# First block of a fused attention and feed-forward kernel: two head pairs normed together in column halves, five groups begun early, sums ahead of products

## The chip, the cores and the metric

The kernel runs on one core of a Trainium2 chip. The metric is the device time of one execution in microseconds, the median over several executions. An execution is also profiled: its span runs from the first to the last instruction of the program on the core, and its time is a little longer than the span.

## The reference

Batch 8, 8 heads, sequence 576, head width 64. Attention without softmax: for each batch and head `kv = k^T v` (64x64), then `out = q kv`, then every row of 64 is divided by its root mean square and scaled by `g_norm`. The heads are laid side by side to `x` of 4608 tokens by 512. A feed-forward layer follows.

```python
kv = np.einsum('bhsd,bhse->bhde', k, v)
out = np.einsum('bhsd,bhde->bhse', q, kv)
rms = np.sqrt(np.mean(out * out, axis=-1, keepdims=True) + 1e-06)
x = (out / rms * g_norm) ...            # heads side by side: 4608 x 512
h = x @ w_in                            # 512 x 2048
g = np.maximum(h, 0.0) + alpha * np.minimum(h, 0.0)
y = g @ w_out                           # 2048 x 512
```

## The kernel before

The 4608 tokens are cut into nine windows of 512 (`W`). The 8 heads are taken as four pairs of 128 columns, `j` 0 to 3, which are also the four chunks `c` of the 512 columns of `x`. The 2048 columns of `w_in` are 16 groups `g` of 128. All products are in fp16 with fp32 sums in PSUM. The order of every engine's work is the order in which the kernel writes it out: each engine runs its own instructions in that order and waits on semaphores of the others. An instruction that waits holds up all that is behind it on its engine.

Loads go through GpSimd's queue, which casts to fp16: q, k, v of batch 0 in halves of four heads, then `w_in` in four quarters of four groups each (`load_w_in`), then k and q of batch 1, a quarter of `w_out`, v of batch 1, the other three quarters of `w_out`, then batch 2. GpSimd issues them in that order, and may have only a few under way: from the ninth on, it waits for an earlier one to land.

For the first two windows the attention is done column-wise by pairs. `regroup` (L106) copies q or k on VectorE into the order that TensorE reads. `step_t` (L211, L220) transposes q of a pair by five products into PSUM and copies it to SBUF on VectorE. `step_kv` (L232, L236) makes kv of two pairs and masks it to two diagonal blocks. `step_ot` (L257, L263) multiplies to `ot_ps` (128 columns of the pair by 512 tokens) and squares it on ScalarE. `ssq_mm` (L273, L275, L278) sums the squares over each head's 64 columns by a product with the mask, then takes ln and exp on ScalarE to get `rstd`. `norm` (L284) multiplies `ot_ps`, `g` and `rstd` on VectorE to `xt`, the pair's chunk of `x`.

A group of the first layer (`m1_group`) is four products over `c` into a PSUM bank `h_ps` (L422), then `m1_evac`: relu of the negative on ScalarE (`m_sb`, L429) and a multiply-add on VectorE (`gt`, L431). The second layer sums 16 groups into a bank (`y_mm`, L444). [...]

The first window is the part that changes. Before, it does pairs 0 and 1, then pairs 2 and 3; it begins three groups on pairs 0 and 1 in the three `h` banks, ends them when pairs 2 and 3 are normed, and then does groups 3 to 15 one after the other. Around them stand `keep_warm` products (L196), which compute nothing that is used. After group 10 VectorE regroups k of batch 1, after group 12 `spread_g` makes a diagonal of `g` on VectorE (`diag`, L466) and spreads it by a product (`g_ps`, L470; `g_all`, L473), after group 14 VectorE regroups q of batch 1. Then the second layer of window 0 runs three output banks at a time, with the attention of batch 1 put between its products (`window_steps`): the transposes of pair 0 first, then `kv`.

Of the kernel before, what the change touches and what calls it, by code (L numbers as in the profile page):

```python
# [9 lines left out]
FP32 = mybir.dt.float32  # L10
FP16 = mybir.dt.float16
AF = mybir.ActivationFunctionType
ALU = mybir.AluOpType
# [4 lines left out]
def kernel(  # L18
# [11 lines left out]
    nc = tc.nc  # L30

    B, H, S, D = q.shape
# [3 lines left out]
    P = 128  # L36
    NPAIR = H // 2
    W = 512
# [6 lines left out]
    NF = D_FF // P  # L45
    NC = D_MODEL // P
    assert NC == NPAIR and 0 < REM < P
    inv_d = 1.0 / D
    NB_PE = 2

    const_p = ctx.enter_context(tc.tile_pool(name="constp", bufs=1))
    w_p = ctx.enter_context(tc.tile_pool(name="weights", bufs=1))
    xt_p = ctx.enter_context(tc.tile_pool(name="xt", bufs=2))
    xm_p = ctx.enter_context(tc.tile_pool(name="xm", bufs=3))
    qkv_p = ctx.enter_context(tc.tile_pool(name="qkv", bufs=1))
    attn_p = ctx.enter_context(tc.tile_pool(name="attn", bufs=2))
    gt_p = ctx.enter_context(tc.tile_pool(name="gt", bufs=2))
    ysb_p = ctx.enter_context(tc.tile_pool(name="ysb", bufs=4))
    ps_h = ctx.enter_context(tc.tile_pool(name="psh", bufs=3, space=bass.MemoryType.PSUM))
    ps_y = ctx.enter_context(tc.tile_pool(name="psy", bufs=1, space=bass.MemoryType.PSUM))  # L60
    ps_s = ctx.enter_context(tc.tile_pool(name="pss", bufs=1, space=bass.MemoryType.PSUM))
    ps_o = ctx.enter_context(tc.tile_pool(name="pso", bufs=1, space=bass.MemoryType.PSUM))
# [10 lines left out]
            name=nc.get_next_instruction_name(),  # L73
# [31 lines left out]
    def regroup(b, nm, h0=0, h1=H, eng=None):  # L105
        (eng or nc.vector).tensor_copy(  # L106
            out=bufs[b % NBUF][nm][:, :, h0:h1, :].rearrange("p t h d -> p h t d"),
            in_=stages[b % NBUF][nm][:, h0:h1],
        )

    def load_batch(b):
        for nm in ("q", "k", "v"):
            load(b, nm)
# [8 lines left out]
    ident = const_p.tile([P, P], FP32, name="ident")  # L122
# [10 lines left out]
    mask16 = const_p.tile([P, P], FP16, name="mask16")  # L133
# [5 lines left out]
    eps_t = const_p.tile([P, 1], FP32, name="eps_t")  # L139
# [6 lines left out]
    g2col = const_p.tile([P, 1], FP32, name="g2col")  # L146
# [28 lines left out]
    def w_in_blk(c, g):  # L175
        i, r = divmod(g, GW)
        return w_in_sb[i][:, c, r * P : (r + 1) * P]
# [15 lines left out]
    def keep_warm(n, pool=(ps_s, "s")):  # L193
        ps = pool[0].tile([P, W], FP32, name="warm_ps", tag=pool[1])
        for i in range(n):
            nc.tensor.matmul(out=ps[:], lhsT=mask16[:], rhs=warm16[:], start=True, stop=True)  # L196


    qts, kvs, xts = {}, {}, {}
# [4 lines left out]
            return lambda t: st[:, 2 * j : 2 * j + 2, t, :]  # L204
        return lambda t: st[:, t, 2 * j : 2 * j + 2, :]

    def step_t(b, j, pool=(ps_s, "s")):
        qs = pair_cols(b, "q", j)
        qt_ps = pool[0].tile([P, NT * P], FP16, name="qt_ps", tag=pool[1])
        for t in range(NT):  # L210
            nc.tensor.matmul(  # L211
                out=qt_ps[:, t * P : (t + 1) * P],
                lhsT=qs(t),
                rhs=ident16[:],
                is_transpose=True,
                start=(t == 0),
                stop=(t == NT - 1),
            )
        qts[b, j] = attn_p.tile([P, S], FP16, name="qt_sb", tag=f"qt{j}")
        nc.vector.tensor_copy(out=qts[b, j][:], in_=qt_ps[:, 0:S])  # L220

    def step_kv(b, j0=0, j1=NPAIR, pool=(ps_s, "s")):
        if j0 == 0:
# [18 lines left out]
    ots = {}  # L242
    xms = {}

    def xt_of(w, c):
        return xms[w][:, c, :] if w >= NB_PE else xts[w, c][:]

    def step_ot(w, j, pool=None):
        if pool is not None:
            ot_ps = pool[0].tile([P, W], FP32, name="ot_ps", tag=pool[1])  # L250
        else:
            ot_ps = ps_o.tile([P, W], FP32, name="ot_ps", tag=f"o{j % 2}")
        n0 = w * W
        while n0 < (w + 1) * W:
            b = n0 // S
            n1 = min((b + 1) * S, (w + 1) * W)
            nc.tensor.matmul(  # L257
                out=ot_ps[:, n0 - w * W : n1 - w * W], lhsT=kvs[b, j],
                rhs=qts[b, j][:, n0 - b * S : n1 - b * S], start=True, stop=True,
            )  # L260
            n0 = n1
        sq = attn_p.tile([P, W], FP16, name="sq_sb")
        nc.scalar.activation(out=sq[:], in_=ot_ps[:], func=AF.Square)  # L263
        ots[w, j] = (ot_ps, sq)
# [5 lines left out]
    def ssq_mm(w, j, pool=(ps_o, "o2")):  # L270
        ot_ps, sq = ots.pop((w, j))
        ssq_ps = pool[0].tile([P, W], FP32, name="ssq_ps", tag=pool[1])
        nc.tensor.matmul(out=ssq_ps[:], lhsT=mask16[:], rhs=sq[:], start=True, stop=True)  # L273
        rstd = attn_p.tile([P, W], FP32, name="rstd")
        nc.scalar.activation(  # L275
            out=rstd[:], in_=ssq_ps[:], func=AF.Ln, bias=eps_t[:], scale=inv_d,
        )
        nc.scalar.activation(out=rstd[:], in_=rstd[:], func=AF.Exp, bias=0.0, scale=-0.5)  # L278
        ots[w, j] = (ot_ps, rstd)

    def norm(w, j):
        ot_ps, rstd = ots.pop((w, j))
        xts[w, j] = xt_p.tile([P, W], FP16, name="xt", tag=f"xt{j}")
        nc.vector.scalar_tensor_tensor(  # L284
            out=xts[w, j][:], in0=ot_ps[:], scalar=g2col[:], in1=rstd[:],
            op0=ALU.mult, op1=ALU.mult,
        )


    TAIL = NB_PE * (S - W)  # L290
# [126 lines left out]

    gts = {}

    def m1_mm(h_ps, w, g, cs):  # L420
        for c in cs:
            nc.tensor.matmul(  # L422
                out=h_ps[:], lhsT=w_in_blk(c, g), rhs=xt_of(w, c),
                start=(c == 0), stop=(c == NC - 1),
            )

    def m1_evac(h_ps, w, g):
        m_sb = gt_p.tile([P, W], FP32, name="m_sb", bufs=3)
        nc.scalar.activation(out=m_sb[:], in_=h_ps[:], func=AF.Relu, scale=-1.0)  # L429
        gt = gt_p.tile([P, W], FP16, name="gt", tag=f"gt{g}")  # L430
        nc.vector.scalar_tensor_tensor(  # L431
            out=gt[:], in0=m_sb[:], scalar=beta_sb[:, g : g + 1], in1=h_ps[:],
            op0=ALU.mult, op1=ALU.add,
        )
        gts[w, g] = gt

    def m1_group(w, g):
        h_ps = ps_h.tile([P, W], FP32, name="h_ps", tag="h")
        m1_mm(h_ps, w, g, range(NC))
        m1_evac(h_ps, w, g)  # L440

# [17 lines left out]
            nc.sync.dma_start(out=rows[t], in_=y_sb[i : i + REM, :])  # L459

    g_all = const_p.tile([P, D], FP32, name="g_all")

    def spread_g():

        diag = const_p.tile([P, D], FP32, name="diag")
        nc.vector.tensor_scalar(  # L466
            out=diag[0:D], in0=ident[0:D, 0:D], scalar1=g2col[0:D], scalar2=None, op0=ALU.mult,
        )
        g_ps = ps_y.tile([P, D], FP32, name="g_ps", tag="y")
        nc.tensor.matmul(  # L470
            out=g_ps[:], lhsT=ones32[0:D], rhs=diag[0:D], start=True, stop=True,
        )
        nc.vector.tensor_copy(out=g_all[:], in_=g_ps[:])  # L473


    H_POOL = (ps_h, "h")
    keep_warm(10)
    regroup(0, "q", 0, HH)
    step_t(0, 0, H_POOL)
    step_t(0, 1, H_POOL)  # L480
    regroup(0, "k", 0, HH)
    keep_warm(4)
    step_kv(0, 0, 2)
    keep_warm(2)
    step_ot(0, 0)
    step_ot(0, 1)
    regroup(0, "q", HH, H)
    step_t(0, 2, H_POOL)
    step_t(0, 3, H_POOL)
    alpha_ps = ps_y.tile([P, NF], FP32, name="alpha_ps", tag="y")  # L490
    nc.tensor.matmul(
        out=alpha_ps[:], lhsT=alpha_row[:], rhs=ident[0:NF, 0:NF], is_transpose=True,
        start=True, stop=True,
# [3 lines left out]
    nc.vector.tensor_scalar(  # L497
        out=beta_sb[:], in0=alpha_ps[:], scalar1=-1.0, scalar2=1.0, op0=ALU.mult, op1=ALU.add,
    )
    regroup(0, "k", HH, H)  # L500
    ssq_mm(0, 0)
    keep_warm(3)
    ssq_mm(0, 1)
    norm(0, 0)
    keep_warm(3)
    step_kv(0, 2, 4)
    norm(0, 1)
    step_ot(0, 2, (ps_o, "o2"))
    step_ot(0, 3, (ps_y, "y"))
    load_batch(2)  # L510
    first = [ps_h.tile([P, W], FP32, name="h_ps", tag="h") for g in range(3)]
    m1_mm(first[0], 0, 0, (0, 1))
    ssq_mm(0, 2, (ps_s, "s"))
    for g in (1, 2):
        m1_mm(first[g], 0, g, (0, 1))
    ssq_mm(0, 3, (ps_o, "o0"))
    keep_warm(6, (ps_o, "o1"))
    norm(0, 2)
    norm(0, 3)
    for g in range(3):  # L520
        m1_mm(first[g], 0, g, (2,))
    keep_warm(2, (ps_o, "o1"))
    for g in range(3):
        m1_mm(first[g], 0, g, (3,))
        m1_evac(first[g], 0, g)
    for g in range(3, NF):
        m1_group(0, g)
        if g == 10:
            regroup(1, "k")
        if g == 12:  # L530
            spread_g()
        if g == 14:
            regroup(1, "q")
# [31 lines left out]
    for w in range(1, NW):  # L565
        steps = phase_steps(w + 1)
        for g in range(NF):
# [12 lines left out]
            if parts[0] == 0:  # L580
                pool, tag = ((ps_y, "y"), (ps_s, "s"))[a % 2 if w > 1 else 0]
                y = pool.tile([P, W], FP32, name="y_ps", tag=tag)
# [10 lines left out]
    for a in range(TPW):  # L593
        y = ps_h.tile([P, W], FP32, name="y_ps", tag="h")
# [33 lines left out]
```

## Time and profile before

| | |
|---|---|
| median of four runs | 302.3 us (301.56, 302.02, 302.57, 303.42) |
| the profiled execution | 302.57 us, span 300.6 us |
| mean granted TensorE clock | 0.990 |
| TensorE busy (matmul) | 284.4 us, 95% of the span |
| VectorE, ScalarE, GpSimd busy | 166.9, 153.0, 97.9 us |
| read from HBM, written | 36.71 MB, 9.44 MB |

The times of the lines below are those of one execution, the profiled one. Busy TensorE time counts overlapped products, so 95% does not say that it runs at its peak. The granted clock is the share of TensorE's full clock that the chip allowed in a stretch.

### The profile page before, as it was taken

To read this page: it belongs to the slowest core of one execution; us is meant where nothing else is said; L and a number is where in the kernel's file an instruction comes from. 1 tells how busy PE (TensorE), PEld (TensorE's weight loads), DVE (VectorE), ACT (ScalarE), POOL (GpSimd) and SP (SyncE) were. 2 spreads that over 40 slices of the span, in tenths; PEclk is the share of its full clock that TensorE was granted. 3 is DMA by queue.
4 is the path that set the end of the run, shared out by engine and by line. 5 is a ranking of instruction groups with operands and counts; after the bars stand their busy time and mean duration, and the time that the engine had idled before them with its cause. 6 is when DMAs were issued, how large, how long until landed. Compare 5 with 4: busy or idle time off the path is not lost.

```text
span 300.6 us, 4238 instructions
## 1 busy us (share of the span) xinstructions
PE 284.4 (95%) x1530; PEld 136.5 (45%) x1530; DVE 166.9 (56%) x255; ACT 153.0 (51%) x298; POOL 97.9 (33%) x109
## 2 busy tenths in 40 slices
PE   5889799889999999999999999999999999999993
PEld 2434254444554454445544544454445444444441
DVE  5548654587695458445954584368537743443200
ACT  1376317774684457435843663467347544434220
POOL 9923410546046615541556166315002200000000
PEclk9999899999999999999999999999999999999998
DMA  7999999999139954992399449926211411122133
GB/s 91 193 206 200 203 204 188 170 210 171 41 76 128 230 110 81 153 234 62 81 137 221 106 80 179 215 53 92 58 35 39 94 35 35 38 51 53 38 70 70
DMA packets 66068, 35.54 MB, mean 118 GB/s; under 512 B 32752, under 2 KB 61440, under 8 KB 66048
## 3 DMA queue, kind: packets, MB, share of 16 engines
q0 software_dynamic: 29664, 18.35, 43.5%
q1 hardware_dynamic: 36384, 16.93, 28.2%
q8 instruction: 12, 0.20, 0.3%
q14 instruction: 8, 0.07, 0.1%
HBM read 36.71 MB, written 9.44 MB: 154 GB/s over the span
## 4 chain that ended last, share of the span: by engine, by line
PE 87%; DVE 3%; ACT 3%; issue 2%; DMA 2%; POOL 2%; POOLq 0%; ACTq 0%
PE h_ps L422 39%; PE y_ps L444 37%; PE kv_ps L232 3%; PE otm_ps L340 2%; DMA vst<-in_v_dram 2%; DVE gt L431 1%; PE warm_ps L196 1%; ACT m_sb L429 1%; PE ssq_ps L273 1%; ACT rstd L275 1%; PE ya L444 1%; PE yb L444 1%; PE yc L444 1%; PE ot_ps L257 1%; DVE ksb L106 1%
## 5 line engine op out<-in xcount | busy, mean ns | idle before, releaser
L431 DVE SCALAR_TENSOR_TENSOR gt<-m_sb,beta_sb,h_ps 128x512 f16<-128x512 f32 x144 | 106.8, 745 | 82.3 <-ACT m_sb L429 81.2
L444 PE MATMUL y_ps<-w_out_sb,gt 128*128 128x512 f16 x528 | 134.9, 379 | 0.0
L429 ACT ACTIVATE m_sb<-h_ps 128x512 f32<-128x512 f32 x144 | 85.6, 597 | 92.1 <-PE h_ps L422 92.0
L422 PE MATMUL h_ps<-xm,w_in_sb 128*128 128x512 f16 x448 | 115.0, 379 | 0.0
L444 PEld LDWEIGHTS <-gt 128*128 128x128 f16 x576 | 56.0, 98 | 65.8 <-issue 1.5
L422 PEld LDWEIGHTS <-w_in_sb 128*128 128x128 f16 x576 | 55.2, 98 | 64.5 <-issue 4.9
L364 POOL TENSOR_TENSOR rg<-ss,g_all 128x512 f32<-128x512 f32 (+1 forms) x30 | 31.2, 1041 | 86.9 <-ACT ss L362 86.0
L422 PE MATMUL h_ps<-xt,w_in_sb 128*128 128x512 f16 x128 | 32.9, 395 | 2.1 <-DVE gt L431 2.1
L451 ACT COPY y_sb<-y_ps 128x512 f32<-128x512 f32 x33 | 19.2, 581 | 17.4 <-PE y_ps L444 17.4
L352 DVE TENSOR_REDUCE ss<-sqm_sb 128x8 f32<-128x512 f32 (+1 forms) x30 | 20.5, 682 | 9.6 <-ACT sqm_sb L346 9.5
L346 ACT ACTIVATE sqm_sb<-otm_ps 128x512 f32<-128x512 f32 (+1 forms) x30 | 17.8, 592 | 9.3 <-PE otm_ps L340 9.3
L373 DVE TENSOR_TENSOR xrow<-otm_ps,rg 128x512 f16<-128x512 f32 (+1 forms) x30 | 20.4, 681 | 3.6 <-POOL rg L364 3.6
L106 POOL COPY qsb<-qst 128x2560 f16<-128x2560 f16 x5 | 11.6, 2316 | 11.9 <-issue 9.3
L106 POOL COPY ksb<-kst 128x2560 f16<-128x2560 f16 x5 | 11.6, 2318 | 7.3 <-DMA kst<-in_k_dram 7.3
L196 PE MATMUL warm_ps<-warm,mask 128*128 128x512 f16 x30 | 9.7, 461 | 3.8 <-DVE eps_t L140 3.3
L340 PEld LDWEIGHTS <-qtm 128*128 128x128 f16 x120 | 9.2, 98 | 8.4 <-issue 1.5
L340 PE MATMUL otm_ps<-kv_sb,qtm 128*128 128x128 f16 x120 | 11.6, 219 | 1.2 <-DVE xm L314 1.2
L263 ACT ACTIVATE sq_sb<-ot_ps 128x512 f16<-128x512 f32 x8 | 4.5, 589 | 15.4 <-PE ot_ps L257 15.4
L232 PE MATMUL kv_ps<-vst,ksb 128*128 128x128 f16 x160 | 10.4, 219 | 1.1 <-DMA vst<-in_v_dram 0.6
L232 PEld LDWEIGHTS <-ksb 128*128 128x128 f16 x160 | 9.5, 98 | 4.1 <-DVE ksb L106 2.0
L284 DVE SCALAR_TENSOR_TENSOR xt<-ot_ps,g2col,rstd 128x512 f16<-128x512 f32 x8 | 6.0, 749 | 8.9 <-ACT rstd L278 8.9
L359 ACT ACTIVATE ss<-ss,eps_t 128x8 f32<-128x8 f32 (+1 forms) x30 | 9.0, 301 | 3.1 <-DVE ss L352 3.1
(62 smaller groups left out, 124.2 us busy)
## 6 DMA issues: line engine op xcount, KB each, us to landing
out_dram<-y_sb SPq DMA_DIRECT2D x72, 128.0 KB, 2.4
kst<-in_k_dram POOLq DMA_DIRECT2D x7, 320.0 KB, 7.9
qst<-in_q_dram POOLq DMA_DIRECT2D x7, 320.0 KB, 5.0
vst<-in_v_dram POOLq DMA_DIRECT2D x7, 320.0 KB, 9.8
w_in_sb<-in_moe_w_in_dram POOLq DMA_DIRECT2D x4, 512.0 KB, 10.2
w_out_sb<-in_moe_w_out_dram POOLq DMA_DIRECT2D x4, 512.0 KB, 15.3
kst<-in_k_dram POOLq DMA_DIRECT2D x7, 256.0 KB, 8.9
qst<-in_q_dram POOLq DMA_DIRECT2D x7, 256.0 KB, 6.5
```

Of the source, the lines that this page charges most:

```text
L106: (eng or nc.vector).tensor_copy(out=bufs[b % NBUF][nm][:, :, h0:h1, :].rearrange("p t h d -> p h t d"), in_=stages[b % NBUF][nm][:, h0:h1],)
L232: nc.tensor.matmul(out=kv_ps[:, j - j0, :], lhsT=ks(t), rhs=vs(t), start=(t == 0), stop=(t == NT - 1),)
L340: nc.tensor.matmul(out=ot_ps[:, 2 * j : 2 * j + 2, :], lhsT=qtms[b][:, t * NPAIR + j, :], rhs=kvs[b, j], start=True, stop=True,)
L346: nc.scalar.activation(out=sq[0:n], in_=ot_ps[0:n], func=AF.Square)
L352: nc.vector.tensor_reduce(out=ss[0:n], in_=sq[0:n], op=ALU.add, axis=mybir.AxisListType.X,)
L364: nc.gpsimd.tensor_tensor(out=rg[0:n], in0=ss[0:n].unsqueeze(2).to_broadcast([n, H, D]), in1=g_all[0:n].unsqueeze(1).to_broadcast([n, H, D ...
L373: nc.vector.tensor_mul(out=x[0:n], in0=ot_ps[0:n], in1=rg[0:n])
L422: nc.tensor.matmul(out=h_ps[:], lhsT=w_in_blk(c, g), rhs=xt_of(w, c), start=(c == 0), stop=(c == NC - 1),)
L429: nc.scalar.activation(out=m_sb[:], in_=h_ps[:], func=AF.Relu, scale=-1.0)
L431: nc.vector.scalar_tensor_tensor(out=gt[:], in0=m_sb[:], scalar=beta_sb[:, g : g + 1], in1=h_ps[:], op0=ALU.mult, op1=ALU.add,)
L444: nc.tensor.matmul(out=y[:], lhsT=gts[w, g][:, a * P : (a + 1) * P], rhs=w_out_blk(g), start=(g == 0), stop=(g == NF - 1),)
L451: nc.scalar.copy(out=y_sb[:], in_=y[:])
```

## The change

In the order in which it stands in the kernel:

- The copy of the transposed q of pair 1 goes from VectorE to ScalarE (`eng=nc.scalar`).
- The sums of squares of pairs 0 and 1 are put earlier in TensorE's order: that of pair 0 ahead of the transposes of pairs 2 and 3, that of pair 1 ahead of the regroup of k. The warm products become fewer (30 become 21), some in the bank `o2`.
- Pairs 2 and 3 are no longer squared, summed and normed one after the other with 512 tokens each, but together, 256 tokens of both at a time: `half_ot` and `half_ssq`. The squares of the first half are made on ScalarE, those of the second on VectorE by a copy and a multiply.
- Five groups are begun, not three: two in the banks `o0` and `o1`. Their products on pair 0 stand partly ahead of and partly between `half_ot` and `half_ssq`; those on pair 1 between the two sums. The products on pairs 2 and 3 are done in halves of 256 columns, for the first half of all five groups, then for the second, then the groups are evacuated.
- Groups 5 and 6 use the banks `s` and `y`; from group 7 on the three `h` banks rotate.
- `diag` is made right after the first five groups, not in `spread_g`.

```diff
-        nc.vector.tensor_copy(out=qts[b, j][:], in_=qt_ps[:, 0:S])
+        if eng is nc.scalar:
+            nc.scalar.copy(out=qts[b, j][:], in_=qt_ps[:, 0:S])
+        else:
+            nc.vector.tensor_copy(out=qts[b, j][:], in_=qt_ps[:, 0:S])
...
+    HW = W // 2
+
+    def half_ot(i, pool, eng=None):
+        ot_ps = pool[0].tile([P, 2, HW], FP32, name="ot_ps", tag=pool[1])
+        for u in range(2):
+            nc.tensor.matmul(
+                out=ot_ps[:, u, :], lhsT=kvs[0, 2 + u],
+                rhs=qts[0, 2 + u][:, i * HW : (i + 1) * HW], start=True, stop=True,
+            )
+        sq = attn_p.tile([P, 2, HW], FP16, name="sq_sb")
+        if eng is nc.vector:
+            o_sb = attn_p.tile([P, 2, HW], FP32, name="o_sb", tag="rg")
+            nc.vector.tensor_copy(out=o_sb[:], in_=ot_ps[:])
+            nc.vector.tensor_mul(out=sq[:], in0=ot_ps[:], in1=o_sb[:])
+        else:
+            nc.scalar.activation(out=sq[:], in_=ot_ps[:], func=AF.Square)
+        ots["half", i] = (ot_ps, sq)
+
+    def half_ssq(i, pool):
+        ot_ps, sq = ots.pop(("half", i))
+        ssq_ps = pool[0].tile([P, 2, HW], FP32, name="ssq_ps", tag=pool[1])
+        nc.tensor.matmul(out=ssq_ps[:], lhsT=mask16[:], rhs=sq[:], start=True, stop=True)
+        rstd = attn_p.tile([P, 2, HW], FP32, name="rstd")
+        ...                                        # Ln, Exp on ScalarE as in ssq_mm
+        for u in range(2):
+            if i == 0:
+                xts[0, 2 + u] = xt_p.tile([P, W], FP16, name="xt", tag=f"xt{2 + u}")
+            nc.vector.scalar_tensor_tensor(
+                out=xts[0, 2 + u][:, i * HW : (i + 1) * HW], in0=ot_ps[:, u, :],
+                scalar=g2col[:], in1=rstd[:, u, :], op0=ALU.mult, op1=ALU.mult,
+            )
...
-    step_t(0, 1, H_POOL)
+    step_t(0, 1, H_POOL, nc.scalar)
     regroup(0, "k", 0, HH)
-    keep_warm(4)
+    keep_warm(4, O2)
     step_kv(0, 0, 2)
-    keep_warm(2)
+    keep_warm(1, O2)
     step_ot(0, 0)
     step_ot(0, 1)
     regroup(0, "q", HH, H)
+    ssq_mm(0, 0)
     step_t(0, 2, H_POOL)
     step_t(0, 3, H_POOL)
...
+    ssq_mm(0, 1)
+    keep_warm(3)
     regroup(0, "k", HH, H)
-    ssq_mm(0, 0)
-    keep_warm(3)
-    ssq_mm(0, 1)
     norm(0, 0)
-    keep_warm(3)
+    keep_warm(2)
     step_kv(0, 2, 4)
-    norm(0, 1)
-    step_ot(0, 2, (ps_o, "o2"))
-    step_ot(0, 3, (ps_y, "y"))
     load_batch(2)
     first = [ps_h.tile([P, W], FP32, name="h_ps", tag="h") for g in range(3)]
-    m1_mm(first[0], 0, 0, (0, 1))
-    ssq_mm(0, 2, (ps_s, "s"))
-    for g in (1, 2):
-        m1_mm(first[g], 0, g, (0, 1))
-    ssq_mm(0, 3, (ps_o, "o0"))
-    keep_warm(6, (ps_o, "o1"))
-    norm(0, 2)
-    norm(0, 3)
+    first += [ps_o.tile([P, W], FP32, name="h_ps", tag=f"o{g}") for g in range(2)]
     for g in range(3):
-        m1_mm(first[g], 0, g, (2,))
-    keep_warm(2, (ps_o, "o1"))
-    for g in range(3):
-        m1_mm(first[g], 0, g, (3,))
-        m1_evac(first[g], 0, g)
-    for g in range(3, NF):
-        m1_group(0, g)
+        m1_mm(first[g], 0, g, (0,))
+    half_ot(0, (ps_s, "s"))
+    norm(0, 1)
+    half_ot(1, (ps_y, "y"), nc.vector)
+    for g in (3, 4):
+        m1_mm(first[g], 0, g, (0,))
+    half_ssq(0, O2)
+    for g in range(5):
+        m1_mm(first[g], 0, g, (1,))
+    keep_warm(1, O2)
+    half_ssq(1, O2)
+    for i in range(2):
+        for c in (2, 3):
+            for g, h_ps in enumerate(first):
+                m1_mm(h_ps, 0, g, (c,), slice(i * HW, (i + 1) * HW))
+                if (i, c) == (1, 3):
+                    m1_evac(h_ps, 0, g)
+    nc.vector.tensor_scalar(
+        out=diag[0:D], in0=ident[0:D, 0:D], scalar1=g2col[0:D], scalar2=None, op0=ALU.mult,
+    )
+    for g in range(5, NF):
+        m1_group(0, g, {5: (ps_s, "s"), 6: (ps_y, "y")}.get(g, H_POOL))
```

More of the change, by code (lines that the diff above doesn't have):

```diff
@@ L205, in pair_cols, with step_t @@
         return lambda t: st[:, t, 2 * j : 2 * j + 2, :]
-    def step_t(b, j, pool=(ps_s, "s")):
+    def step_t(b, j, pool=(ps_s, "s"), eng=None):
         qs = pair_cols(b, "q", j)
@@ L287, in norm @@
         )
+    HW = W // 2
[19 more added lines that the diff above has]
+        rstd = attn_p.tile([P, 2, HW], FP32, name="rstd")
+        nc.scalar.activation(
+            out=rstd[:], in_=ssq_ps[:], func=AF.Ln, bias=eps_t[:], scale=inv_d,
+        )
+        nc.scalar.activation(out=rstd[:], in_=rstd[:], func=AF.Exp, bias=0.0, scale=-0.5)
+        for u in range(2):
[5 more added lines that the diff above has]
+            )
     TAIL = NB_PE * (S - W)
@@ L418, with m1_mm @@
     gts = {}
-    def m1_mm(h_ps, w, g, cs):
+    def m1_mm(h_ps, w, g, cs, cols=slice(0, W)):
         for c in cs:
             nc.tensor.matmul(
-                out=h_ps[:], lhsT=w_in_blk(c, g), rhs=xt_of(w, c),
-                start=(c == 0), stop=(c == NC - 1),
+                out=h_ps[:, cols], lhsT=w_in_blk(c, g), rhs=xt_of(w, c)[:, cols],
+                start=(c == 0), stop=(c == NC - 1 and cols.stop == W),
             )
@@ L435, in m1_evac, with m1_group @@
         gts[w, g] = gt
-    def m1_group(w, g):
-        h_ps = ps_h.tile([P, W], FP32, name="h_ps", tag="h")
+    def m1_group(w, g, pool=(ps_h, "h")):
+        h_ps = pool[0].tile([P, W], FP32, name="h_ps", tag=pool[1])
         m1_mm(h_ps, w, g, range(NC))
@@ L461 @@
     g_all = const_p.tile([P, D], FP32, name="g_all")
+    diag = const_p.tile([P, D], FP32, name="diag")
     def spread_g():
[L465 to L468, printed above, removed]
         g_ps = ps_y.tile([P, D], FP32, name="g_ps", tag="y")
@@ L476 @@
     H_POOL = (ps_h, "h")
+    O2 = (ps_o, "o2")
     keep_warm(10)
@@ L499 @@
     )
+    ssq_mm(0, 1)
+    keep_warm(3)
     regroup(0, "k", HH, H)
-    ssq_mm(0, 0)
-    keep_warm(3)
-    ssq_mm(0, 1)
     norm(0, 0)
-    keep_warm(3)
+    keep_warm(2)
     step_kv(0, 2, 4)
-    norm(0, 1)
-    step_ot(0, 2, (ps_o, "o2"))
-    step_ot(0, 3, (ps_y, "y"))
     load_batch(2)
     first = [ps_h.tile([P, W], FP32, name="h_ps", tag="h") for g in range(3)]
-    m1_mm(first[0], 0, 0, (0, 1))
-    ssq_mm(0, 2, (ps_s, "s"))
-    for g in (1, 2):
-        m1_mm(first[g], 0, g, (0, 1))
-    ssq_mm(0, 3, (ps_o, "o0"))
-    keep_warm(6, (ps_o, "o1"))
-    norm(0, 2)
-    norm(0, 3)
-    for g in range(3):
-        m1_mm(first[g], 0, g, (2,))
-    keep_warm(2, (ps_o, "o1"))
-    for g in range(3):
-        m1_mm(first[g], 0, g, (3,))
-        m1_evac(first[g], 0, g)
-    for g in range(3, NF):
-        m1_group(0, g)
+    first += [ps_o.tile([P, W], FP32, name="h_ps", tag=f"o{g}") for g in range(2)]
+    for g in range(3):
+        m1_mm(first[g], 0, g, (0,))
[17 more added lines that the diff above has]
+        out=diag[0:D], in0=ident[0:D, 0:D], scalar1=g2col[0:D], scalar2=None, op0=ALU.mult,
+    )
+    for g in range(5, NF):
+        m1_group(0, g, {5: (ps_s, "s"), 6: (ps_y, "y")}.get(g, H_POOL))
         if g == 10:
```

## The prediction

> **What bounds the kernel now.** I read the page first, then the chain of waits around the change, then the stages of the run cut at the changes of the granted clock, then the timelines of the engines in the first block. The page says that the run as a whole belongs to TensorE:
>
> ```profile
> span 300.6 us, 4238 instructions
> PE 284.4 (95%) x1530; PEld 136.5 (45%) x1530; DVE 166.9 (56%) x255; ACT 153.0 (51%) x298; POOL 97.9 (33%) x109
> PEclk9999899999999999999999999999999999999998
> ```
>
> The fifth slice of the clock row, 30 to 37.5 us, is below full. The chain of waits shows what happens there (columns: start, us, what):
>
> ```profile
> 22.99 7.08 PE h_ps L422 x32
> ...
> 31.39 0.82 DVE ksb L106
> 32.21 1.32 DVE gt L431 x2
> 33.53 0.17 DVE diag L466
> ...
> 33.73 0.43 PE g_ps L470 x2
> 34.17 4.40 PE h_ps L422 x12
> ...
> 40.38 1.29 PE kv_ps L232 x20
> ```
>
> VectorE regroups k of batch 1, then makes gt 11 and 12, then diag; TensorE, which ran out of work after group 12, waits for diag (1.95 us by the list of waits). Then twelve products take 4.40 us, though four take 0.86 elsewhere. The stages, cut at the clock's changes, say why (columns: stage, its length, PE, PEld, DVE, ACT and POOL busy, granted clock, DMA):
>
> ```profile
> 31.57:34.98 3.41, 1.46 (x9) 0.71 (x8) 2.34 (x5) 0.60 (x1) 1.59 (x2) 1.00 1.36 199
> 34.98:38.40 3.42, 3.42 (x10) 1.21 (x9) 1.61 (x3) 1.19 (x2) 1.35 (x2) 0.50 1.26 206
> 58.87:62.29 3.42, 2.22 (x17) 1.19 (x16) 2.48 (x4) 2.35 (x5) 1.61 (x3) 1.00 1.20 184
> ```
>
> TensorE was busy 1.46 of 3.41 us (43%), and the next stage of the same length ran at clock 0.50. A stage with 2.22 busy (65%) had no such sequel. So the limit lies between 43% and 65%; half clock over 3.41 us costs 1.7 us of full TensorE work. The profiled execution (302.57 us, span 300.6) holds this loss once. It lies 0.27 us above the median of the four runs, 302.3; the runs lie 1.86 us apart, about what one such loss is worth, so I take the executions to differ in it.
>
> What releases the first block is the arrival of the weights, to be read from GpSimd, which waits for one of its transfers before it issues the next:
>
> ```profile
> 17.09 0.77 POOL L169 DMA_DIRECT2D w_out_sb<-in_moe_w_out_dram  x1 [1.74 <-DMA w_in_sb<-in_moe_w_in_dram]
> 19.62 0.69 POOL L96 DMA_DIRECT2D vst<-in_v_dram  x1 [1.76 <-DMA w_in_sb<-in_moe_w_in_dram]
> ```
>
> The first quarter of w_in (groups 0 to 3) is there at about 16.8 us, the second (groups 4 to 7) at about 19.35. The wait sits some 0.28 us ahead of each issue: 9.31 + 7.5, the shortest landing of w_in, is 16.81.
>
> **The change, part by part.** Durations are rows of the profile: a 512-column product every 0.216 (four in 0.86), Ln 0.68, Exp 0.63, gt 0.75, but 0.66 from start to start where gts are ready (three in 2.06), m_sb 0.60. A half norm (128x256) is not in the trace. By the kv_sb rows (512 columns 0.692, 256 columns 0.424) a half saves 0.27, so 0.48 against the 0.75 of the whole; the bounds are 0.38 (half) and 0.75. A half product is 0.11 (half of 0.216). ScalarE's copy of qt_sb is bounded by 0.45 (VectorE's) and 0.65 (ScalarE's y_sb copy, scaled to 576 columns), VectorE's copy of o_sb from below by 0.45 and from above by 0.69 (kv_sb at 512). None of these three is on the path: the copies end before 10 and 19.7 us, and their readers wait for weights or for ssq.
>
> *Up to 16.8 us: nothing.* The qt copy on ScalarE, the earlier sum, the warm products taken out (30 become 21) let TensorE finish kv of pairs 2 and 3 near 15.0, where it now ends at 15.7. But the next instruction in TensorE's queue is now the product of group 0 on pair 0, which needs the first quarter: TensorE stands until 16.9. What is queued behind it is half_ot(0). Today the ot of pairs 2 and 3 start at 16.24, ahead of the weights; then they start at 16.9 + 3 x 0.216 = 17.55, a loss of 1.3 us.
>
> *16.9 to 24.6 us.* The four half ot end at 18.0; Square (0.59) ends at 18.6. TensorE does group 3, then reaches the c = 0 product of group 4 and stands until the second quarter, 19.45. Behind it waits the first half's sum: 19.67, its result 20.05. Today that sum starts at 17.32. Ln and Exp end at 21.45, the two half norms, 0.40 apart, at 22.35. The second sum follows five products and a warm one (19.9 + 1.3 = 21.2, result 21.6); Ln, Exp, 22.95; half norms at 23.45 and 23.85. TensorE has the ten half products of the first half done by then and does the second half from 23.5, pair 3 from 24.05 to 24.6. The first m_sb starts at 24.35 and the first gt at 24.97, against 22.19 now. But five groups are then done, not three: TensorE starts group 5 at 24.6 and ends it at 25.5, where it is today as well (its m_sb starts at 25.78).
>
> *24.6 to 38.6 us.* TensorE is level, VectorE is late: gt k starts at 24.97 + 0.66 k, diag takes 0.11 more after gt 4. Groups 5 to 9 have free PSUM banks and end at 28.9. Group 10 takes the bank of group 7, whose gt ends at 24.97 + 4.62 + 0.11 + 0.75 = 30.45: a new stall of 1.6 us. Then gt is no longer behind. Groups 10 to 12 end at 33.1; diag is long there, so the wait of 1.95 us is gone; g_ps takes 0.43; group 13 ends at 34.4. VectorE: gt 10 until 32.9, ksb until 33.7, gt 11 until 34.3, gt 12 until 35.0; group 14 and 15 pass with no wait above 0.1, and the first y product starts at 36.1 (38.37 now). Next late is VectorE again: gt 14 until 36.8, qsb until 37.5, then the transposes of pair 0, gt 15 until 38.2, the copy of qt until 38.6, and kv of batch 1 starts at 38.6 instead of 40.38. **The sum so far: 1.8 us earlier, clock untouched.**
>
> *What the 1.8 us meets.* GpSimd's queue issues the same transfers in the same order, each as an earlier one lands; DMA moves 184 to 206 GB/s in the stages quoted, from 31 us to 62, so landings stay. v of batch 1 is issued at 19.62 and 22.17, longest landing 15.5: by 37.7, in time. v of batch 2, second part, 39.28 + 13.7 (the median of these early ones) = 53.0, needed at 55.40 - 1.8 = 53.6: covered by 0.6 us; if the cover goes, the gain shrinks one for one. SP's transpose of q follows its regroup. Behind that, up to the end, TensorE is the bound, so the shift stays: 302.57 - 1.8 = 300.8.
>
> *The clock.* TensorE now stands from 15.0 to 16.9 and from about 18.2 to 19.45. In the profiled execution's stages (14.50 to 17.92), it would be busy some 1.5 of 3.41 us, 44 to 49%; a stage that holds both gaps has 2.1 us idle, 38% busy, less than the 43% that dropped. A drop in 17 to 21 us doubles the product of group 4, the first sum, the five products and the second sum: about eight products of 0.216, of which the part inside the stage counts, 0.6 to 1.7 us by where it lies, 0.9 in the profiled execution's. That gives 301.4 to 302.5, likeliest 301.6.
>
> The row says that a gap of 1.95 us is enough to lose the clock. [...]
>
> **The rivals.** (a) *The clock holds* through 15 to 21 us, because the limit is nearer to 43% or the gaps fall into two stages: 300.8, and 300.1 with shorter half norms and a shorter stall. For it: 44 to 49% lies above the one stage that dropped. Against: every stage that holds both gaps lies below it. (b) *Slower: a second drop at the bank stall.* TensorE idle from 28.9 to 30.5 leaves a stage around it 53% busy; if the limit is above 53%, as 65% allows, the next 3.4 us run at half clock and cost 1.7 more: 301.7 + 1.7 = 303.4, up to 304.5 where the first drop costs its most. It decides from a stall of 1.2 us (65% busy) if the limit is there. Against: 53% is nearer to the middle than either row. (c) *No difference*: VectorE or the v of batch 2 takes the gain back, 302.4; for it, the cover of 0.6 us only.
>
> **How the numbers follow.** The forecast has 0.38, (a) 0.36, (b) 0.19, (c) 0.07. The bound of what a measurement tells from no change, 0.5%, is 1.5 us: 300.8 and 303.8. Faster: 0.27 of (a), which lies at this bound and takes all that my sums count too long, and 0.02 of the forecast: 0.29. Slower: 0.14 of (b). Within: 0.57. The range leaves out 0.08 of (a) below 300.4 and 0.11 of (b) above 303.6. The forecast's own range is 301.2 to 302.5.
>
> **What would show it.** Right: first gt near 25 us, group 10 waiting for a gt near 29, no wait for diag, y from 36 to 37, kv of batch 1 from 38.6 to 39.7, clock 0.50 once near 17 to 21 and not after 33. Wrong: the sum of the first half before 19.4, an ot of pair 2 before 16.8, or kv of batch 1 after 40.4.

## The result, and the profile after

| | before | after |
|---|---|---|
| median of the runs shown with the result | 302.13 us (79 runs, 301.16 to 304.33) | 301.52 us (53 runs, 300.71 to 302.72) |
| profiled execution, span | 302.57, 300.6 us | 301.03, 299.0 us |
| first gt of the first block | 22.19 | 25.07 |
| first product of the second layer (y) | 38.37 | 36.28 |
| kv of batch 1, of batch 2, of batch 3 (first product) | 40.38, 55.40, 77.66 | 38.81, 53.82, 76.08 |

The ratio is 0.9972, with a 95% interval from 0.9964 to 0.998: faster by 0.28%, within the 0.5% that counts as no change here. Ratios here and below come from comparable runs on the same chip, so they are not the quotients of the medians. The shift at kv of batch 1, 1.57 us in the two profiled executions, is still there at batch 2 (1.58), at batch 3 (1.58) and in the span (1.6).

The page of the kernel after (span; busy time, share and instructions of each engine; the granted clock in 40 slices):

```profile
span 299.0 us, 4244 instructions
PE 281.5 (94%) x1533; PEld 136.4 (46%) x1533; DVE 167.1 (56%) x258; ACT 153.0 (51%) x298; POOL 97.6 (33%) x109
PEclk9999999999999999999999999999999999999999
```

TensorE has three instructions more and is busy 2.9 us less: the clock row has no slice below its highest digit (9 is 90% or more). The chain of waits of the kernel after, from the weights to kv of batch 2 (start, us, what):

```profile
10.05 9.21 DMA w_in_sb<-in_moe_w_in_dram
19.30 0.39 PE h_ps L461
19.69 0.22 PE ssq_ps L314
...
25.07 3.38 DVE gt L470 x5
...
30.63 2.75 PE h_ps L461 x12
33.38 0.36 PE g_ps L506 x2
33.75 1.85 PE h_ps L461 x8
...
53.82 1.29 PE kv_ps L235 x20
```

The first half's sum runs behind the product of group 4, which is what the second quarter of w_in releases at 19.30. The five evacuations then stand in a row on VectorE. At 33.38 `g_ps` follows the products of groups 10 to 12 with nothing between: the wait for `diag` is gone, and eight products behind it take 1.85 us, where twelve took 4.40 at half clock. TensorE's timeline of the kernel after shows the two gaps in front of the weights and the stall at group 10 (start, us, line, operation, tiles, count; in brackets the idle time before it and its releaser):

```profile
13.46 1.46 PE L196 MATMUL warm_ps<-warm,mask 128*128 128x512 f16 x5
14.98 0.72 PE L235 MATMUL kv_ps<-vst,ksb 128*128 128x128 f16 x10
16.80 0.82 PE L461 MATMUL h_ps<-xt,w_in_sb 128*128 128x512 f16 x3 [1.11 <-DMA w_in_sb<-in_moe_w_in_dram]
...
19.30 0.39 PE L461 MATMUL h_ps<-xt,w_in_sb 128*128 128x512 f16 x1 [1.03 <-DMA w_in_sb<-in_moe_w_in_dram]
19.53 0.38 PE L314 MATMUL ssq_ps<-sq_sb,mask 128*128 128x512 f16 x1
...
30.63 2.75 PE L461 MATMUL h_ps<-xt,w_in_sb 128*128 128x512 f16 x12 [1.47 <-DVE gt L470]
```

The stages of the kernel after that hold these gaps, cut like those of before (stage, its length, PE, PEld, DVE, ACT and POOL busy, granted clock, DMA):

```profile
14.48:17.89 3.41, 2.25 (x19) 1.34 (x18) 1.36 (x3) 0.63 (x2) 1.44 (x2) 1.00 1.24 207
17.89:21.30 3.41, 2.32 (x12) 0.84 (x10) 1.38 (x2) 1.90 (x3) 0.69 (x1) 1.00 1.24 206
28.13:31.54 3.41, 1.94 (x10) 0.82 (x9) 3.41 (x7) 2.15 (x4) 1.66 (x3) 1.00 1.34 203
```

TensorE is busy for 66%, 68% and 57% of them, and the clock stays at 1.00 behind each.

### The profile page after: what moved, and what is told of

It reads as the page before. It is cut to its first block, busy times and chain, and to the rows that moved or that the text cites. A ratio compares the mean times of both kernels' runs of the same rounds, so it can differ in the third digit from the quotient of the medians.

```text
span 299.0 us, 4244 instructions
## 1 busy us (share of the span) xinstructions
PE 281.5 (94%) x1533; PEld 136.4 (46%) x1533; DVE 167.1 (56%) x258; ACT 153.0 (51%) x298; POOL 97.6 (33%) x109
## 4 chain that ended last, share of the span: by engine, by line
PE 83%; DVE 4%; POOL 3%; ACT 3%; DMA 3%; issue 2%; POOLq 0%; ACTq 0%
PE y_ps L483 38%; PE h_ps L461 37%; DMA w_in_sb<-in_moe_w_in_dram 3%; PE kv_ps L235 3%; PE otm_ps L379 2%; DVE gt L470 2%; PE yc L483 1%; PE yb L483 1%; PE ya L483 1%; ACT m_sb L468 1%; PE qt_ps L211 0%; POOL qst L96 0%; ACT rstd L278 0%; PE ssq_ps L276 0%; POOL qst L100 0%
## 5 line engine op out<-in xcount | busy, mean ns | idle before, releaser
L461 PEld LDWEIGHTS <-w_in_sb 128*128 128x128 f16 x586 | 55.8, 98 | 66.0 <-issue 4.9
L461 PE MATMUL h_ps<-xt,w_in_sb 128*128 128x512 f16 (+1 forms) x138 | 31.6, 364 | 5.4 <-DVE gt L470 2.6
L196 PE MATMUL warm_ps<-warm,mask 128*128 128x512 f16 x21 | 7.6, 498 | 3.3 <-DVE eps_t L140 3.3
L239 DVE TENSOR_TENSOR kv_sb<-kv_ps,mask 128x512 f16<-128x512 f32 (+1 forms) x9 | 5.6, 628 | 4.1 <-PE kv_ps L235 4.0
L96 POOL DMA_DIRECT2D vst<-in_v_dram x9 | 6.6, 728 | 2.9 <-DMA w_in_sb<-in_moe_w_in_dram 1.7
```

What stands on the lines that cost most here:

```text
L461: nc.tensor.matmul(out=h_ps[:, cols], lhsT=w_in_blk(c, g), rhs=xt_of(w, c)[:, cols], start=(c == 0), stop=(c == NC - 1 and cols.stop == W),)
```

## The experiments

The questions were: which part of the change brings the gain (`diag`, or the new order of the first block); what half clock is worth and what sets it off; and what limits the gain further on. The first four are cut so that each does or undoes one thing.

### 1. `diag` alone

Before, with `diag` made behind the first three groups, and nothing else of the change:

```diff
-        nc.vector.tensor_scalar(out=diag[0:D], ...)    # in spread_g, after group 12
+    nc.vector.tensor_scalar(out=diag[0:D], ...)        # ahead of the loop over groups 3 to 15
```

> The kernel before, with diag made right after the first three groups and nothing else changed. Theory D (the gain is diag's: its wait of 1.95 us and the clock lost behind it go, and the new first block by itself costs): TensorE goes from group 12 to g_ps with no wait, y starts near 34.6, kv of batch 1 near 37.1 (40.38 before, 38.81 after), then kv of batch 2 stands until its v lands at 53.0, so that only some 0.9 us are left against an undropped run of before: median 300.6 us, 1.5 below before's and 0.9 below the changed kernel's. Theory B (the new first block brings the gain, diag is by the way): between before and after, 301.8 us.

Measured: 301.14 us (12 runs, 300.44 to 303.64), ratio 0.9954 [0.9933, 0.9975]. The one small instruction brings about as much as the whole change: the intervals of the two overlap. The profiled execution, 302.33, shows where it ends. Its load stream ran late (`w_in`'s first quarter is there at 18.7 us where it is at 16.6 to 17.5 in the others), and yet the y products begin at 36.52. Then the chain of waits is one of transfers up to kv of batch 2 (start, us, what):

```profile
12.79 14.34 DMA w_in_sb<-in_moe_w_in_dram
27.41 13.56 DMA w_out_sb<-in_moe_w_out_dram
41.25 13.83 DMA vst<-in_v_dram
55.21 1.28 PE kv_ps L232 x20
```

Each is issued when an earlier one lands; v of batch 2 lands last. TensorE was at kv of batch 1 by 39.05 us, 1.33 ahead of before, and is 0.19 ahead at kv of batch 2.

### 2. The change without its `diag`

After, with `diag` put back into `spread_g` (the diff above, the other way round).

> The changed kernel with diag back in spread_g, behind gt 12 on VectorE. Theory D: TensorE waits for diag again, longer than before since VectorE is later (its gts started 2.9 us later): y near 38.2, kv of batch 1 near 40.7, median 303.0 us and up to 304.5 where the clock drops, slower than before by 0.9 or more. Theory B: 301.5 to 302.0 us, still faster than before.

Measured: 304.99 us (7 runs, 304.18 to 305.33), ratio 1.0065 [1.0042, 1.0088]: slower than before. The chain of waits of this kernel (start, us, what):

```profile
32.95 0.82 DVE ksb L106
33.77 1.31 DVE gt L470 x2
35.09 0.17 DVE diag L505
35.30 0.43 PE g_ps L509 x2
35.73 4.38 PE h_ps L461 x12
```

Since gt runs later in the new block, `diag` behind two gts and the regroup is later too, 35.09 against 33.53, and the wait drops the clock as it did before. Its stages:

```profile
32.90:36.31 3.41, 1.46 (x8) 0.60 (x6) 2.57 (x6) 0.81 (x2) 1.36 (x2) 1.00 1.36 201
36.31:39.72 3.41, 3.41 (x9) 1.21 (x8) 1.14 (x2) 1.19 (x2) 0.94 (x2) 0.50 1.24 207
```

1.46 of 3.41 us busy, then 0.50: the same pair of rows as in the kernel before. But an earlier stage of the same execution, into which most of both gaps in front of the weights falls, is as little busy (1.47 us, 43%), and the clock holds behind it:

```profile
15.82:19.24 3.42, 1.47 (x8) 0.70 (x8) 2.11 (x4) 0.60 (x1) 0.76 (x1) 1.00 1.24 206
19.24:22.65 3.41, 2.94 (x16) 1.49 (x17) 1.23 (x3) 2.15 (x4) 1.08 (x2) 1.00 1.24 207
```

The y products start at 39.95, 1.58 later than before. So the new first block by itself costs time at that point, and `diag` pays for it.

### 3. The wait kept, the clock held

Before, with eight warm products put into the wait:

```diff
         if g == 12:
+            keep_warm(8, (ps_o, "o1"))
             spread_g()
```

> The kernel before with eight warm products ahead of g_ps, in the time in which TensorE waits for diag. If the clock's drop behind the wait is what spreads the runs of before (301.2 to 304.3): the wait for diag stays at some 0.2 us of idle with 1.7 us of useless products, the clock stays at 1.00 from 35 to 38 us, y starts near 36.7, and the runs lie at 301.5 us with none above 302.5. If the spread has another cause: median 302.1 us and the same spread as before.

Measured: 301.92 us (12 runs, 301.47 to 302.45), ratio 0.9975 [0.9957, 0.9993]. TensorE's timeline and the stage behind the wait, of this kernel:

```profile
31.77 1.89 PE L196 MATMUL warm_ps<-warm,mask 128*128 128x512 f16 x8
33.89 0.43 PE L470 MATMUL g_ps<-diag,ones 64*128 64x64 f32 x2 [0.23 <-DVE diag L466]
```

```profile
34.98:38.40 3.42, 3.10 (x15) 1.15 (x14) 2.33 (x4) 1.79 (x3) 2.13 (x3) 1.00 1.26 206
```

`g_ps` starts no earlier than before (33.89), only the clock behind it is full, and kv of batch 1 comes at 39.38 instead of 40.38: the drop costs 1.0 us there. From 39.38 to the 38.81 of the kernel after, 0.57 us are left for all else that the change does. This splits the spread of before as well. Of its 87 executions beside these experiments, 42 have a mean granted clock of 0.9945 or less and a median of 303.17 us; 45 have 0.9975 or more and a median of 302.07; none lie between. With the warm products none is above 302.45. Of the kernel after, 4 of 54 are at 0.9945 or less, and the other 50 have a median of 301.46. The mean clock also counts half clock behind the last product, where it costs nothing (the last 2.8 us of the span in the profile of before), so those 4 are the most that can have had a drop. So about 0.6 us of the gain does not depend on the drop, and about 1.1 us more is there against the half of the executions of before that have it.

### 4. The sums ahead of the products that wait for weights

After, with the ot of both halves ahead of the products on pair 0, and the first sum right behind the four products that the first quarter of `w_in` allows:

```diff
-    for g in range(3):
-        m1_mm(first[g], 0, g, (0,))
     half_ot(0, (ps_s, "s"))
     norm(0, 1)
     half_ot(1, (ps_y, "y"), nc.vector)
-    for g in (3, 4):
+    for g in range(4):
         m1_mm(first[g], 0, g, (0,))
     half_ssq(0, O2)
-    for g in range(5):
+    for g in range(4):
         m1_mm(first[g], 0, g, (1,))
     keep_warm(1, O2)
     half_ssq(1, O2)
+    m1_mm(first[4], 0, 4, (0, 1))
```

> The changed kernel with TensorE's order in the first block changed alone: half_ot ahead of the products on pair 0, which wait for the first quarter of w_in; the products of group 4, which wait for the second quarter, behind both sums. Theory Q (the new block's cost is what its sums wait for in TensorE's queue, the two quarters): the first sum starts near 18 us instead of 19.53, the first gt near 23.1 instead of 25.07, the bank stall at group 10 shrinks, y near 34.2, kv of batch 1 near 36.8; then v of batch 2 binds at 53.0: median 300.6 us. Theory H (the halves themselves, more and shorter instructions, are the cost): first gt 24.5 or later, median 301.3 us or more.

Measured: 301.44 us (12 runs, 300.29 to 302.96), ratio 0.9954 [0.9933, 0.9976]. In the first block it does what was expected: the first gt at 23.18 us (25.07 after), y at 34.39 (36.28), kv of batch 1 at 36.91 (38.81). Little of these 1.9 us is left in the time. TensorE's timeline of this kernel, and the stages around the second line:

```profile
17.77 0.38 PE L314 MATMUL ssq_ps<-sq_sb,mask 128*128 128x512 f16 x1
...
53.51 2.12 PE L235 MATMUL kv_ps<-vst,ksb 128*128 128x128 f16 x20 [1.95 <-DMA vst<-in_v_dram]
```

```profile
50.31:53.73 3.42, 1.48 (x11) 0.65 (x10) 2.23 (x3) 2.05 (x5) 0.00 (x0) 1.00 1.34 183
53.73:57.14 3.41, 3.41 (x27) 2.58 (x25) 0.69 (x1) 0.60 (x1) 1.14 (x3) 0.50 1.05 239
```

The sum moves from 19.53 to 17.77, and the 1.9 us come back as a wait of 1.95 us for v of batch 2. In this execution that wait drops the clock in its turn (mean clock 0.993; so in four of the twelve, 302.2 to 303.0 us; the other eight have a median of 300.86, so there some of the gain is left). v of batch 2 lands at 53.4 us here (issued at 39.04, 14.33 us to landing) and at 53.0 in the kernel after, although TensorE is 1.9 us earlier at kv of batch 1, so what is won ahead of 53.4 us ends there.

### 5, 6, 7. The consumer of that load moved back

kv of batch 2 two steps later in window 1, in the kernels of 1 and 4 and in the kernel after:

```diff
-            steps[0][1].append(lambda: step_kv(w))
+            steps[2 if w == NB_PE else 0][1].append(lambda: step_kv(w))
```

> The kernel before with diag early, as in the first of these runs, and in window 1 step_kv of batch 2 in the third step instead of the first, two groups later. Theory L (with diag early the kernel stands at kv of batch 2 until the last v of batch 2 lands, 53 to 55 us by the execution, and that is what caps every gain in the first block): the stand goes, kv of batch 2 runs near 54 with groups done ahead of it, and the median falls to 299.1 us, with less spread. Rival K (the chain behind kv, ScalarE, VectorE and GpSimd from 56 to 68 us, takes it back): 300.6 us or more.

> The changed kernel with the sums first in TensorE's queue, as in the fourth of these runs, and step_kv of batch 2 two groups later. Theory L: 298.8 us, 0.3 below the run with diag alone and the same move, which is what the new first block is worth once its queue order is mended. Rival K: 300.6 us or more. If the new first block is worth nothing even so: the same as the run with diag alone, within 0.2.

> The changed kernel with step_kv of batch 2 two groups later and nothing else. Theory L: its kv of batch 2 starts at 53.8 us, about when the last v lands, so the landing hardly binds and the move gives little: 0.3 to 0.5 us, median 301.1. Rival: the move itself is the gain wherever it is made: 299.5 us.

| | kv of batch 1 | span | median | ratio |
|---|---|---|---|---|
| 5: `diag` alone, kv later | 37.74 | 298.5 | 300.45 us (6 runs) | 0.9924 [0.9898, 0.9951] |
| 6: sums first, kv later | 37.13 | 298.0 | 300.36 us (6 runs) | 0.9925 [0.9899, 0.9952] |
| 7: after, kv later | 39.33 | 299.2 | 301.17 us (12 runs) | 0.9962 [0.9944, 0.998] |

Number 7 gains next to nothing over the kernel after, whose kv of batch 2 did not wait for v (a wait of 0.4 us in front of it is for VectorE's regroup). Numbers 5 and 6 beat both kernels, and they are level: the new first block with its order mended is worth nothing measurable over `diag` alone. They fell short of what was expected, 299.1 for number 5. The chain of waits of number 5 shows the next limit (start, us, what):

```profile
56.42 0.18 POOL gate L555
...
56.92 0.69 POOL qst L96
...
60.33 0.68 POOL vst L100
61.01 1.85 POOL rg L364 x2
```

GpSimd waits at its gate until the transposes of q of batch 2 are there, issues six transfers of batch 3, and only then multiplies `rg` for the rows of the next window. Number 6 has the same chain: the gate at 55.91, `rg` at 60.45.

### 8. Without the warm products in front of kv of pairs 2 and 3

After, with five warm products taken out of the first block:

```diff
     ssq_mm(0, 1)
-    keep_warm(3)
     regroup(0, "k", HH, H)
     norm(0, 0)
-    keep_warm(2)
     step_kv(0, 2, 4)
```

> The changed kernel without the five warm products ahead of kv of pairs 2 and 3, so that TensorE stands from 13.5 to 14.4 and from 15.1 to 16.8 us. If the clock drops behind stages of 3.41 us that are busy less than about 45%, as the one stage of before (43%) and the changed kernel's (57 to 68%, no drop) say: clock 0.50 for 3.41 us somewhere from 16 to 22 us in most executions, the doubled products cost 0.2 to 1.7 us by where they lie, median 301.9 us and a spread up to 303.2. If it takes a whole idle stage: no drop, 301.5 us or a little less.

Measured: 301.97 us (12 runs, 301.01 to 302.99), ratio 0.9978 [0.9957, 0.9998], 0.45 us above the kernel after by the medians; the intervals of the two ratios overlap, so in the time this is not clear of the noise. The stages of its profiled execution (302.43):

```profile
11.60:15.02 3.42, 1.86 (x19) 1.16 (x18) 2.56 (x6) 3.36 (x6) 3.12 (x6) 1.00 1.34 199
15.02:18.43 3.41, 2.13 (x13) 1.04 (x11) 1.08 (x2) 0.18 (x1) 1.33 (x2) 0.50 1.24 206
18.43:21.84 3.41, 3.41 (x12) 1.37 (x11) 1.38 (x2) 1.69 (x3) 0.69 (x1) 0.50 1.24 205
```

The drop that the prediction put at 17 to 21 us comes here, from 15.0 to 21.8, and in 11 of the 12 runs the mean clock is 0.994 or less. kv of batch 1 is at 40.21, 1.4 us later than in the kernel after; 0.3 of that is a later load stream (the first product on weights at 17.08 instead of 16.80). kv of pairs 2 and 3 does start earlier without the warm products, at 14.76 instead of 14.98, and what it waits for in this execution is the landing of v:

```profile
14.76 1.04 PE L235 MATMUL kv_ps<-vst,ksb 128*128 128x128 f16 x10 [1.03 <-DMA vst<-in_v_dram]
```

### 9, 10. Without the gate

The kernels of 6 and 5 without GpSimd's copy that waits for the transposes:

```diff
-            gate = const_p.tile([1, 1], FP16, name="gate")
-            nc.gpsimd.tensor_copy(out=gate[:], in_=qtms[2][0:1, 0, 0:1])
             load_batch(3)
```

> The kernel of the sixth run (sums first, kv of batch 2 two groups later) without the gate, the small copy on GpSimd that waits until the transposed q of batch 2 has landed before batch 3's loads are issued. Theory G (with kv out of the way, the next that ends last is GpSimd: gate at 55.9 us, six issues until 60.45, only then the first rg, for which VectorE's xrow and behind it the gt wait): the issues are done before 53 us, the first rg starts near 58.5, kv of batch 3 near 74 instead of 75.08, median 299.3 us. Rival C: batch 3's loads, now under way beside the transposes of batch 2's q, make those land later than 55.86 us, tile_a of batch 2 waits, and the median is 300.4 us or more.

> The same without the gate on the kernel of the fifth run (before, diag early, kv of batch 2 two groups later, the old first block). Theory G: 299.5 us, level with the run with the new first block within 0.3, since what the first block wins is covered by landings. Rival C: 300.4 us or more.

Measured: 308.62 us (5 runs), ratio 1.0199 [1.0174, 1.0224], and 308.40 us (6 runs), ratio 1.0193 [1.0169, 1.0218]. Without the gate they are 2.0% and 1.9% slower than before. The chain of waits of number 9:

```profile
48.29 16.05 DMA qtm<-qsb
64.39 0.61 PE otm_ps L379 x4
```

With the loads of batch 3 issued beside them, the transposes of q land at 64.34 us instead of 55.86, TensorE waits 9.0 us for them, and the clock is at 0.50 from 57.9 to 68.1.

### 11, 12. The gate kept, the six transfers spread out

The kernels of 6 and 5 with the loads of q, k and v of batch 3 each behind one of the first three `rg` of window 1:

```diff
-            load_batch(3)                              # behind the gate
...
+            if w == 1 and g in (3, 4, 5):
+                load(3, "qkv"[g - 3])
```

> The kernel of the sixth run (sums first, kv of batch 2 two groups later), the gate kept, and batch 3's loads issued one tensor at a time behind the first three rg on GpSimd instead of all six issues ahead of them. Theory G (in the sixth run the six issues, 56.4 to 60.45 us, hold the first rg up by 1 to 2 us): the first rg starts near 59, kv of batch 3 near 74, median 299.5 us. Rival P (batch 3's k and v now land 4 us later, after 70 us, and GpSimd stands at their regroups or TensorE at kv of batch 3): 300.4 us or more.

> The same on the kernel of the fifth run (before with diag early, kv of batch 2 two groups later, the old first block). Theory G: 299.7 us. Rival P: 300.4 us or more. The two runs of this call side by side say what the new first block with its sums first is worth once nothing behind it covers it: 0.3 us by the sixth run's expectation, 0 by its result.

Measured: 302.59 us (12 runs), ratio 1.0013 [0.9991, 1.0035], and 302.72 us (12 runs), ratio 1.001 [0.9989, 1.003]: the gain of 6 and 5 is lost. The first `rg` does come earlier, but only by 0.80 us (59.65 against 60.45), since it now waits for ScalarE's `ss`, its own input. Then the chain of waits of number 11 says:

```profile
66.27 10.03 DMA xm<-xrow
...
76.44 1.04 PE h_ps L461 x4
```

Of the three transposes of the next window's rows (`xm`) that begin here, the shortest lands in 6.2 us, the longest in 10.0; in number 6, where batch 3's loads were issued earlier, it is 5.6 and 6.9. TensorE waits 1.8 us for the last of them. Number 12's chain has the same transfer (10.21 us, landing at 76.44); TensorE waits only 0.3 us for it there, since the clock was at 0.50 from 67.0 to 70.4 us. It was not tried to issue the loads in yet another place, so what would take the time below 300.4 us stays open.

## Why the prediction was right, and where it was not

**The time, 301.6 against 301.52: right, with one term of its sum wrong.** The sum was 302.57 - 1.8 + 0.9, that is 301.67, put down as 301.6. The first term was 1.57 in the profiled executions. The second was nothing there.

**The path from the sums to kv of batch 1: right.** First sum put at 19.67, came at 19.53; first gt 24.97, 25.07; stall at group 10 1.6 us, 1.47; y 36.1, 36.28; kv of batch 1 38.6, 38.81. The half norm, which the trace of before did not show, was put at 0.48 and 0.40 from start to start; VectorE's two in a row take 0.88.

**The clock drop in the first block: wrong, and it is the step that failed.** I let TensorE end kv of pairs 2 and 3 near 15.0 us and stand until 16.9, 1.9 us, and took 0.9 us for the drop that follows. It ended at 15.70, stood 1.11 us, and no drop came. What held kv were the warm products ahead of it. TensorE's lines in the kernel before:

```profile
13.93 0.38 PE L273 MATMUL ssq_ps<-sq_sb,mask 128*128 128x512 f16 x1
14.14 0.81 PE L196 MATMUL warm_ps<-warm,mask 128*128 128x512 f16 x3
15.01 0.72 PE L232 MATMUL kv_ps<-vst,ksb 128*128 128x128 f16 x10
```

In the kernel after, the same sum on TensorE (the warm products and kv behind it are in the timeline above, at 13.46 and 14.98), and the issue of the last part of v on GpSimd:

```profile
13.25 0.38 PE L276 MATMUL ssq_ps<-sq_sb,mask 128*128 128x512 f16 x1
```

```profile
8.48 0.61 POOL L100 DMA_DIRECT2D vst<-in_v_dram  x1
```

The sum comes 0.68 us earlier, but five warm products stand between it and kv, where there were three, and they take 1.46 us: kv starts at 14.98 instead of 15.01. I counted the warm products taken out of the whole block, not those that stand ahead of kv. The landing of v did not hold it here: issued at 8.48, with 5.7 us to landing, v was there at about 14.2. It is the next limit behind the warm products, as number 8 shows, where v was issued at 8.27 and landed 6.4 us later.

With gaps of 1.11 and 1.03 us the stages were 66% and 68% busy, and rival (a)'s case came: its 300.8 stands against 301.03 in the profiled execution. But the shorter gap is not the whole answer. In number 2 a stage was 43% busy because of these two gaps, close to the case that I had feared, and the clock held, though it dropped behind another stage of 43% in the same execution. So a low busy share, on which I built the 0.9 us, was not enough for a drop there; why not is open.

The median lies 0.5 above that execution, though at least 50 of 54 show no drop; executions of one kernel differ by other things too. In number 1 it was a late load stream; what it is in the kernel after, one profile does not show. So two errors, a drop that didn't come and a profile taken for typical (it holds the drop that only half of the executions of before have), cancel in the number: that the forecast hits so closely is luck.

**The mechanism of the drop: right in part.** Number 8 makes the longer gaps and gets the drop, for 0.45 us by the medians, which is not clear of the noise; the prediction had 0.6 to 1.7, and the profiled execution of number 8 lost 1.4 at kv of batch 1, 0.3 of it to its later load stream. In the profiled execution of before, half clock came behind a wait of 1.95 us, and 42 of the 87 executions of before have a mean clock of 0.9945 or less. In that of number 8 it came behind a gap of 1.03 us and lasted across the next, of 1.28 us; 11 of the 12 runs have a mean clock of 0.994 or less. In the kernel after, gaps of 1.11 and 1.03 us stand at about the same place, and the clock is 1.00 in their stages and behind them. So gaps of one to two microseconds were enough here, and the length of a gap alone did not decide. Why about half of the executions of before drop, and half do not, no run here shows.

**The bank stall, rival (b): it came (1.47 us, a stage 57% busy), and the clock held.** That speaks for a limit below 57% there. But it isn't a sharp share by the trace's busy time: the first stage of number 8 was 54% busy and dropped, and in number 2 a stage from 15.82 to 19.24, busy 1.47 of 3.42 us, did not. What decides it is open.

**The cover of 0.6 us at v of batch 2: right, and it turned out to be the main limit.** I used it for a small rival (c) only. In the kernel after, the 1.57 us fit under it: v lands at 53.0, and kv starts at 53.82. Number 4 shows what lies beyond: 1.9 us more ahead of it, and a wait of 1.95 us in front of it.

**What the prediction did not ask: which part brings the gain.** It counted the change as one sum. Numbers 1 and 2 part it: `diag`'s new place alone brings about as much as the whole change, and without it the new block costs. At the first y product, with a normal load stream, `diag` alone (number 5) is at 35.04 and the kernel after at 36.28. The sums of the kernel after stand in TensorE's queue behind products that wait for the second quarter of weights. Number 4 takes that away, and then numbers 5 and 6 are level: at the end nothing measurable is left to win.

## What to carry to other kernels

Where an engine waits for a small operation whose inputs have long been ready, move that operation ahead first and time it alone: here one instruction of 0.17 us did what a new order of a whole block did. Before an early gain is counted, find the transfer that lands next behind it, and the slack in front of it: here the last v of batch 2 landed at 53.0 us in the kernel after and at 53.4 in number 4, and the 1.9 us that number 4 won ahead of it came back as a wait of 1.95 us. In a queue that runs in order, as TensorE's did here, put what a long chain waits for ahead of work that waits for a load (in number 4 this brought the first gt from 25.07 to 23.18 us), and do not take it that the clock survives a gap of one or two microseconds: it did behind gaps of 1.11 and 1.03 us in the kernel after, and did not behind one of 1.95 us in the kernel before and one of 1.03 us in number 8.

## What the runs showed of the hardware

- Half clock comes or stays away by the execution: 42 of 87 runs of the kernel before show it by a mean clock of 0.9945 or less, at about 1.1 us each (medians of 303.17 and 302.07 us), and at most 4 of 54 of the kernel after.
- The transposes of q of batch 2 by DMA took 16.05 us with the loads of batch 3 issued beside them (number 9), 7.6 us where the gate held these back (number 6).
- The start of the load stream moves from execution to execution: the first quarter of `w_in` was there at 16.8 us in the profiles of before and after, and at 18.7 in that of number 1, with the same loads in the same order.
